# Gate and value by 16 block products for 18, over two token groups, with the tap products on ScalarE

## The chip, the cores and the metric

One Trainium2 chip, one core of it. The time is that of one execution on the device, in microseconds (us); a run gives several, and the median of the fast ones is quoted. The kernel before takes 3069 us, and its runs agree within 0.2%. The engines are named as in the profile: PE is TensorE's matmul, PEld its weight load, DVE is VectorE, ACT ScalarE, POOL GpSimd, SP SyncE, which here only starts DMAs (transfers between DRAM and the chip's memory). PSUM is the memory, in banks, in which TensorE adds up its products; reading a finished bank out is an eviction.

## The reference

A causal convolution with 7 taps, softmaxed for each of 8 heads, then an RMS norm and a SwiGLU layer without bias, on 8 sequences of 4096 tokens, 192 channels, 1536 inner columns, in fp32. The three weight matrices arrive as 64-bit floats; both kernels convert them to fp32 on the chip, once, by arithmetic on their 32-bit halves. This is the "conversion" of the start.

```python
# cut to what matters
w = softmax(weight, axis=-1)                         # (8 heads, 7 taps)
y[b, s, h*24:(h+1)*24] = sum_k w[h, k] * x_padded[b, s + k, h*24:(h+1)*24]
xn = y / sqrt(mean(y*y, axis=-1) + 1e-6) * rms_g      # 32768 tokens x 192
g, v = xn @ w_gate, xn @ w_val                        # 192 -> 1536 each
out = (silu(g) * v) @ w_out                           # 1536 -> 192
```

## The kernel before

A group is 512 tokens. The 192 channels are three blocks of 64, and TensorE works as two halves of 64 rows: the gate weights lie in the lower partitions, the value weights in the upper ones, so a gate product and a value product run side by side (the prediction shows the numbers).

```python
# cut to what matters
def load(g):                      # x of a group: a row of the tile holds 4 tokens and 6 before them
    ...
    src = bass.AP(tensor=row.tensor, offset=row.offset,
                  ap=[[NJ * D, P - first], [D, NJ + HALO], [1, D]])
    nc.sync.dma_start(out=t[first:, :, :], in_=src)     # first = 2 at the start of a sequence

# front(g), step by step beside the products of the group before
for k in range(K):                # both the tap products and the sums on VectorE (k = 0 only fills y)
    nc.vector.tensor_tensor(out=m[:], in0=xk, in1=w, op=ALU.mult)
    nc.vector.tensor_tensor(out=y[:], in0=y[:], in1=m[:], op=ALU.add)
...                               # squares, root, scaling, transpose, through DRAM

# inner(g): 12 column blocks, 3 channel blocks, gate and value
for c in range(NC):
    for ps, rows in ((gate, LOW), (val, UPP)):
        nc.tensor.matmul(out=ps[:], lhsT=w_in[rows, c, f * P : (f + 1) * P],
                         rhs=xg[rows, c, :], start=(c == 0), stop=(c == NC - 1))
nc.scalar.activation(out=sg[:], in_=gate[:], func=AF.Silu)
nc.vector.tensor_tensor(out=ht[:, f, :], in0=val[:], in1=sg[:], op=ALU.mult)

# outer(g, ht): 4 x 12 x 2 products of 192 columns, two evictions, one store
```

## Time and profile before

| | before |
|---|---|
| time, median | 3069.3 us |
| span of the profiled run | 3067.6 us |
| TensorE busy | 2990.7 us (97%) |
| VectorE, ScalarE, GpSimd busy | 51%, 20%, 3% |
| two groups (1024 tokens), steady | 93.0 us |
| first two groups done at | 179.7 us |

It is read from the top: who is busy, who is on the chain that ended last, at what rate the steady part runs, and what the start costs apart from that. The lines stand in the prediction below.

### The profile page before, as it was taken

What the parts mean: (1) busy time and instruction counts of PE and PEld (TensorE: products, weight loads), DVE (VectorE), ACT (ScalarE), POOL (GpSimd) and SP (SyncE); (2) the same over time, 40 slices, a digit from 0 to 9 for tenths busy, and PEclk for the clock granted to TensorE, in tenths of its full rate; (3) what the DMA queues carried; (4) which work ended last, traced back from release to release, by engine and by line L of the source; (5) the groups of instructions that cost most, each with busy time, mean ns of one, the idle gap of its engine ahead of it and who ended that gap; (6) DMA issues with size and microseconds to landing.
All of it is one profiled execution on the core that took longest, in us unless ns stands there. A gap on an engine that the chain in (4) does not pass through costs nothing.

```text
span 3067.6 us, 49649 instructions
## 1 busy us (share of the span) xinstructions
PE 2990.7 (97%) x21504; PEld 1896.0 (62%) x21504; DVE 1572.0 (51%) x2176; ACT 625.4 (20%) x1423; POOL 93.7 (3%) x163
## 2 busy tenths in 40 slices
PE   2799999999999999999999999999999999999999
PEld 1465665665665666666656656656656656666666
DVE  6745545446445455455455455454464454554552
ACT  1212122122122122122122121221221221221221
POOL 1000000000000000000000000000000000000000
PEclk9899999999999999999999999999999999999999
DMA  5221212211211211211211112112112112112111
GB/s 121 60 57 51 63 50 57 62 50 52 68 50 52 68 50 52 68 50 52 64 49 56 54 53 62 50 56 64 50 52 68 50 52 68 50 52 68 50 40 27
DMA packets 126731, 173.84 MB, mean 57 GB/s; under 512 B 9520, under 2 KB 91440, under 8 KB 126512
## 3 DMA queue, kind: packets, MB, share of 16 engines
q1 hardware_dynamic: 122880, 163.56, 19.2%
q0 software_dynamic: 1632, 4.72, 0.6%
q8 instruction: 168, 2.75, 0.4%
q10 hardware_dynamic: 2000, 2.39, 0.3%
q14 instruction: 51, 0.42, 0.0%
HBM read 120.31 MB, written 50.33 MB: 56 GB/s over the span
## 4 chain that ended last, share of the span: by engine, by line
PE 96%; DVE 3%; DMA 1%; issue 0%; POOL 0%; ACT 0%; DVEq 0%; SPq 0%; POOLq 0%
PE ps L284 63%; PE ps L302 32%; DMA x_sb<-in_x_dram 1%; DVE m L227 0%; DVE mf L184 0%; DVE sgn L183 0%; DMA raw_out<-in_moe_w_out_dram 0%; DVE y L228 0%; DVE w_in L192 0%; DVE exp L174 0%; DVE ht L290 0%; DVE exp L161 0%; DVE exp L171 0%; DVE sgn L179 0%; DVE man L166 0%
## 5 line engine op out<-in xcount | busy, mean ns | idle before, releaser
L284 PE MATMUL ps<-xT,w_in 64*128 64x512 f32 x9216 | 2002.3, 592 | 71.2 <-DVE sgn L179 47.9
L284 PEld LDWEIGHTS ps<-xT,w_in 64*128 64x128 f32 x9216 | 895.6, 188 | 1134.9 <-issue 1110.1
L302 PEld LDWEIGHTS ps<-wo_sb,ht 64*128 64x128 f32 x12288 | 1002.4, 187 | 31.6 <-issue 30.1
L302 PE MATMUL ps<-wo_sb,ht 64*128 64x192 f32 x12288 | 1009.6, 323 | 0.8 <-DVE wo_sb L189 0.8
L290 DVE TENSOR_TENSOR ht<-ps,sg 128x512 f32<-128x512 f32 x768 | 531.2, 692 | 546.1 <-ACT sg L289 529.2
L289 ACT ACTIVATE sg<-ps 128x512 f32<-128x512 f32 x768 | 458.4, 597 | 1419.0 <-PE ps L284 1410.2
L308 DVE TENSOR_TENSOR o_sb<-ps,o_sb 128x384 f32<-128x384 f32 x128 | 71.4, 558 | 909.0 <-ACT o_sb L307 909.0
L228 DVE TENSOR_TENSOR y<-y,m 128x768 f32<-128x768 f32 x384 | 368.1, 959 | 13.2
L227 DVE TENSOR_TENSOR m<-x_sb,taps 128x768 f32<-128x768 f32 x384 | 364.3, 949 | 0.0
L307 ACT COPY o_sb<-ps 128x384 f32<-128x384 f32 x128 | 61.3, 479 | 929.1 <-PE ps L302 929.1
L240 POOL TENSOR_SCALAR r<-ss 128x4 f32<-128x4 f32 x64 | 12.8, 199 | 2848.4 <-ACT sq L234 2848.4
L258 DVE STREAM_TRANSPOSE nt<-xn 128x768 f32<-128x768 f32 x64 | 99.1, 1548 | 0.0
L234 ACT ACTIVATE sq<-y 128x192 f32<-128x192 f32 x256 | 89.5, 350 | 21.1 <-DVE y L228 14.8
L248 DVE TENSOR_SCALAR xn<-y,r 128x192 f32<-128x192 f32 x256 | 63.8, 312 | 3.0 <-POOL r L243 3.0
L243 POOL TENSOR_TENSOR r<-r,nhalf 128x4 f32<-128x4 f32 x64 | 64.9, 1014 | 5.3
L224 DVE TENSOR_TENSOR y<-x_sb,taps 128x768 f32<-128x768 f32 x64 | 60.2, 941 | 0.0
L234 ACT ACTIVATION_READ_ACCUMULATOR sq<-y 128x1 f32 x256 | 47.6, 186 | 0.0
L170 ACT ACTIVATE mf<-man 128x768 f32<-128x768 uint32 (+1 forms) x12 | 8.2, 683 | 46.4 <-DVE man L166 46.4
L117 POOL DMA_DIRECT2D raw_in<-in_moe_w_val_dram x18 | 9.6, 540 | 40.0 <-DVE mf L184 39.2
L183 DVE TENSOR_TENSOR sgn<-exp,sgn 128x768 uint32<-128x768 uint32 (+1 forms) x12 | 9.1, 759 | 0.4
L76 DVE MEMSET x_sb<- 2x1152 f32 x8 | 8.1, 1018 | 2.3 <-issue 1.2
L192 DVE SCALAR_TENSOR_TENSOR w_in<-mf,rg_sb,sgn 128x256 f32<-128x256 f32 x18 | 7.7, 481 | 0.2
(26 smaller groups left out, 52.8 us busy)
## 6 DMA issues: line engine op xcount, KB each, us to landing
x_sb<-in_x_dram SPq DMA_DIRECT2D x56, 960.0 KB
xT<-xd SPq DMA_DIRECT2D x128, 384.0 KB
xd<-nt SPq DMA_DIRECT2D x256, 96.0 KB
out_dram<-o_sb SPq DMA_DIRECT2D x64, 384.0 KB
x_sb<-in_x_dram SPq DMA_DIRECT2D x8, 945.0 KB
raw_in<-in_moe_w_val_dram POOLq DMA_DIRECT2D x18, 128.0 KB, 7.8
raw_in<-in_moe_w_gate_dram ACTq DMA_DIRECT2D x18, 128.0 KB
raw_out<-in_moe_w_out_dram POOLq DMA_DIRECT2D x12, 192.0 KB, 4.1
```

Source lines behind the costliest of these rows:

```text
L227: nc.vector.tensor_tensor(out=m[:], in0=xk, in1=w, op=ALU.mult)
L228: nc.vector.tensor_tensor(out=y[:], in0=y[:], in1=m[:], op=ALU.add)
L234: nc.scalar.activation(out=sq[:], in_=y[:, j, :], func=AF.Square, accum_out=ss[:, j : j + 1])
L243: nc.gpsimd.tensor_tensor(out=r[:], in0=r[:], in1=nhalf[:], op=ALU.pow)
L248: nc.vector.tensor_scalar(out=n[:, j, :], in0=y[:, j, :], scalar1=r[:, j : j + 1], scalar2=None, op0=ALU.mult,)
L258: nc.vector.transpose(out=nt[:].rearrange("p c b j -> p c j b"), in_=n[:].rearrange("p j (c a) -> p c j a", a=Q),)
L284: nc.tensor.matmul(out=ps[:], lhsT=w_in[rows, c, f * P : (f + 1) * P], rhs=xg[rows, c, :], start=(c == 0), stop=(c == NC - 1),)
L289: nc.scalar.activation(out=sg[:], in_=gate[:], func=AF.Silu)
L290: nc.vector.tensor_tensor(out=ht[:, f, :], in0=val[:], in1=sg[:], op=ALU.mult)
L302: nc.tensor.matmul(out=ps[:, at], lhsT=ht[part, f, j * P : (j + 1) * P], rhs=wo_sb[part, f, :], start=(f == 0), stop=(f == FC - 1),)
L307: nc.scalar.copy(out=o2, in_=low[:, 0 : 2 * D])
L308: nc.vector.tensor_tensor(out=o2, in0=upp[:, 0 : 2 * D], in1=o2, op=ALU.add)
```

## The change

Two groups are taken together as a 2 x 3 array of blocks of x (A1 to A3, B1 to B3), and three column blocks of the weights as a 3 x 3 array. Their product needs 18 block products; a scheme of Strassen's kind needs 16, with sums of blocks of x (8 per pair of groups), sums of blocks of the weights (once, on GpSimd), and with partial sums that are read out of PSUM in the middle of their accumulation and used for several outputs. To make room on VectorE, which reads them, the tap products go to ScalarE, and the scalings by the root with them; four steps of the output weights' conversion go to GpSimd. The core, cut:

```diff
-    T = 512
-    NJ = T // P
+    T = 512
+    PT = 2 * T                       # tokens of a pair of groups
+    NJ = PT // P
 ...
     def load(p):
 ...
-            while first * NJ < HALO:
-                first += 1           # 2: the load is of 126 rows
+            first = 1                # the load is of 127 rows
 ...
     # front(p)
-            nc.vector.tensor_tensor(out=m[:], in0=xk, in1=w, op=ALU.mult)
+            for h in range(H):
+                nc.scalar.mul(m[:, :, hs], t[:, k : k + NJ, hs], taps[:, h, k : k + 1])
+                if h % 2:
+                    yield
             nc.vector.tensor_tensor(out=y[:], in0=y[:], in1=m[:], op=ALU.add)
 ...
+    def unit(u, side):               # 3 column blocks, both groups: 16 products in each half
+        mm(9, d, blk(B3), True)
+        side(1)
+        mm(12, c, cs(SS), True)
+        keep("e", c)                 # ScalarE copies a partial sum to SBUF, both halves
+        side(2)
+        mm(10, d, cs(W))
+        res(3, d, "e", op=ALU.add)   # VectorE: bank + copy, both halves
+        mm(3, a, blk(A3), True)
+        mm(5, a, cs(U))
+        keep("a", a)
+        mm(1, b, blk(A2), True)
+        mm(4, b, cs(U))
+        res(1, b, "a", rev=True)
+        ...                          # GpSimd adds output 3 to the copy "a", both halves
+        mm(13, d, cs(VS))            # the eighth product: into the bank that res(3) has read
+        keep("d2", d)
+        silu(3)
+        ...
 ...
     # main loop: what of the front part of the next pair stands where
+        elif s % 2 == 0:
+            step(nxt)                # in the units of a pair
+        ...
+        if 9 <= s <= 12:             # in its output stage
+            step(sums)               # block sums of x
+        else:
+            step(nxt, 2)
```

The load of x at the start of a sequence has 127 rows. The front part of the next pair has 47 steps, of which two are taken at each of 19 places of the output stage; the last nine are left to the units of the pair that follows.

## The prediction

> **What bounds the kernel now**
>
> I read the busy times first, then the chain that ended last, the groups, the chain in order of time, the timeline of two steady groups, and a table of windows over the start. Busy times, slices and chain, from the page:
>
> ```profile
> PE 2990.7 (97%) x21504; PEld 1896.0 (62%) x21504; DVE 1572.0 (51%) x2176; ACT 625.4 (20%) x1423; POOL 93.7 (3%) x163
> ...
> PE   2799999999999999999999999999999999999999
> ...
> PE 96%; DVE 3%; DMA 1%; issue 0%; POOL 0%; ACT 0%; DVEq 0%; SPq 0%; POOLq 0%
> ```
>
> TensorE is busy all the time after the second slice, and the chain says that it is also what sets the end. VectorE has half its time free, ScalarE four fifths. So fewer products are worth what they cost, as long as nothing else becomes the bound. The groups give the unit costs (columns: line, engine, operation, shapes, count, busy us, mean ns of one, idle before):
>
> ```profile
> L284 PE MATMUL ps<-xT,w_in 64*128 64x512 f32 x9216 | 2002.3, 592 | 71.2 <-DVE sgn L179 47.9
> ...
> L302 PE MATMUL ps<-wo_sb,ht 64*128 64x192 f32 x12288 | 1009.6, 323 | 0.8 <-DVE wo_sb L189 0.8
> L290 DVE TENSOR_TENSOR ht<-ps,sg 128x512 f32<-128x512 f32 x768 | 531.2, 692 | 546.1 <-ACT sg L289 529.2
> L289 ACT ACTIVATE sg<-ps 128x512 f32<-128x512 f32 x768 | 458.4, 597 | 1419.0 <-PE ps L284 1410.2
> ...
> L228 DVE TENSOR_TENSOR y<-y,m 128x768 f32<-128x768 f32 x384 | 368.1, 959 | 13.2
> L227 DVE TENSOR_TENSOR m<-x_sb,taps 128x768 f32<-128x768 f32 x384 | 364.3, 949 | 0.0
> L307 ACT COPY o_sb<-ps 128x384 f32<-128x384 f32 x128 | 61.3, 479 | 929.1 <-PE ps L302 929.1
> ...
> L258 DVE STREAM_TRANSPOSE nt<-xn 128x768 f32<-128x768 f32 x64 | 99.1, 1548 | 0.0
> L234 ACT ACTIVATE sq<-y 128x192 f32<-128x192 f32 x256 | 89.5, 350 | 21.1 <-DVE y L228 14.8
> ...
> L243 POOL TENSOR_TENSOR r<-r,nhalf 128x4 f32<-128x4 f32 x64 | 64.9, 1014 | 5.3
> ```
>
> The program has 4608 gate and value products and the page 9216, so each fp32 product is two instructions; two row halves run side by side, which is why the mean (592) exceeds busy time over count (217). The chain in order of time gives the steady rates:
>
> ```profile
> 1109.74 30.90 PE ps L284 x144
> ...
> 1838.14 15.60 PE ps L302 x192
> ```
>
> 30.90 / 144 = 0.2146 us for each gate or value instruction, 15.60 / 192 = 0.0813 for each output one. A group of 512 tokens takes 46.5 us, two take 93.0. The timeline of VectorE (start us, length us) shows its pitch:
>
> ```profile
> 1112.98 0.69 DVE L290 TENSOR_TENSOR ht<-ps,sg 128x512 f32<-128x512 f32 x1
> 1113.59 0.95 DVE L227 TENSOR_TENSOR m<-x_sb,taps 128x768 f32<-128x768 f32 x1
> 1114.57 0.96 DVE L228 TENSOR_TENSOR y<-y,m 128x768 f32<-128x768 f32 x1
> ```
>
> An operation that needs nothing of its predecessor starts 0.08 us before that one's end (pitch 0.61 for 512 elements); one that needs it starts 0.03 after. The windows 60 to 100 us (columns: PE, PEld, DVE, ACT, POOL, granted clock, DMA) show the start's price:
>
> ```profile
> 60.00:80.00 20.00, 14.15 (x52) 5.90 (x48) 19.59 (x36) 3.78 (x7) 2.66 (x5) 0.83 0.23 59
> 80.00:100.00 20.00, 10.49 (x30) 4.69 (x32) 19.58 (x35) 3.40 (x6) 3.75 (x7) 0.71 0.28 80
> ```
>
> There VectorE is full with the weights' conversion, TensorE waits and its clock falls. The first lasting matmul starts at 53.7 us, and the first two groups end at about 179.7 instead of 93.
>
> **What the Trainium skill says**
>
> "VectorE: DVE Perf Modes", section on the TRN2 errata, gives fp32 tensor_tensor (N+151)/0.96 ns: 691 for 512, and 957 for 768. The trace agrees: 692 and 959. "ScalarE: Activation LUTs", section "What ACT_TABLE_LOAD costs", gives 186 ns + 0.833 N, about 93 more for a per-partition scale, and 93 overlap back to back. For 192 elements that is 346; the trace has 350. A multiplication by a tap is then an estimated 0.44 us at a pitch of 0.35; no run here shows one yet. "GPSIMD Engine Reference", section 3.1, gives about 2.6 cycles per element for a two-input elementwise operation and 4497 ns for 2048; at 1.2 GHz an estimated 1.17 us for 512. The trace has none of that size. "TensorE: Matmul & The Clock Gate", Part 1, says that an idle window of about 3.4 us halves the clock; the falls to 0.83 and 0.71 above come with idle gaps of 3.7 to 5.9 us and agree.
>
> **The change part by part**
>
> 1. Products. A unit (three blocks of 128 gate and value columns, two token groups) has 16 products in each half instead of 18: 32 x 2 x 0.2146 = 13.73 us instead of 15.45. A pair of groups costs TensorE 4 x 13.73 + 2 x 15.60 = 86.1 instead of 93.0. Over 32 pairs that is 220 us, 7.2%, and the ceiling of the gain.
>
> 2. Reading partial sums. VectorE has 12 sums from PSUM and 6 products per unit, where it had 6 products: 18 x 0.61 = 11.0 us in 13.73. ScalarE has 10 copies (estimated 0.58 each, from 479 ns for 384) and 6 Silus: 9.4 us. Both fit, but they are now in a loop with TensorE, because the second product sum into a bank may not start before the first was read.
>
> 3. GpSimd's two sums per unit. They start when the first sum of res1 (the second pair that VectorE reads, ready when the seventh product ends, 6.0 us into the unit) is done, and the next VectorE product (mul3) waits for both: 2 x 1.17 = 2.35 us, with hops 2.45. The other VectorE work of the loop is 17 pitches and an end, 10.45 us. Loop: 12.9 us, below 13.73. So in a unit with nothing else TensorE stays the bound, with about 0.8 us to spare.
>
> 4. The front part. In the page VectorE's tap products (364 us plus 60) and scalings (64) go; ScalarE gets 56 multiplications (19.6 us at 0.35) and 8 scalings per pair. Sums stay on VectorE: 6 x 1.76 us. x block sums add 8 x 0.61 to 0.69. Nearly all of it lies in the output stage of 31.2 us: ScalarE about 24, VectorE about 18. It fits.
>
> 5. What spills over. The side steps are counted out: 38 of 47 front steps fall in the output stage, and the last six only after the last eviction. At the start of the next unit ScalarE evicts (to 0.5 us), does four tap products (1.9), VectorE adds (3.7), then six squares at 0.345 (5.9), and only then comes the copy that res3 needs: res3 ends at 7.7, where the eighth product wanted to start at 6.0. That is 1.7 us of wait. Then squares, the reciprocal root (1.0 on GpSimd, ahead of its two sums) and the eight scalings sit between ScalarE's copies, so mul3 starts at 11.3 instead of 9.2; from there VectorE runs without a gap, with six transposes, 3.3 us, among the sums. res3 of the second unit ends at about 25.0, where TensorE unhindered would want it at 13.73 + 6.0 = 19.7. So a pair loses 5.3 us, which later units cannot give back since TensorE is already full in them. Steady pair: 86.1 + 5.3 = 91.4 against 93.0.
>
> 6. The start. x of 1024 tokens is first (1.4 MB of 6.9 MB; the start before moved 216 to 227 GB/s), tap products from about 17 us, convolution to 39, squares, root and scalings to 46, conversion of the first three blocks to 52, transposes 55, through DRAM and back about 13: first product at about 68, not 54. In pair 0 VectorE has 8.2 us of conversion per unit, 5 of x sums, 14 of front and 10 of output weights beside its 11 per unit: units of about 30, 28, 26 and 14, an output stage of 31, and 8 for waits: pair 0 ends at about 205, where two groups ended at 179.7.
>
> Sum: 205 + 31 x 91.4 + 5 (last eviction and store, 5 before) = 3043.
>
> **The rivals**
>
> A. TensorE stays the bound everywhere and the spill is absorbed: 205 + 31 x 86.1 + 5 = 2879, 6% faster. For it: the busy sums of all engines fit under 86 us. Against it: the queues are in order and only two PSUM banks per running sum are there, so a late copy is a late product.
>
> B. VectorE and GpSimd become the bound in every unit. If a GpSimd sum takes 1.6 us or more, or VectorE's pitch on sums that wait for two engines is 0.70 and not 0.61, the loop is 14.4 us or more: 0.7 x 4 x 31 = 87 us on top, about 3130, slower at the edge. For it: nothing in the trace shows this GpSimd operation.
>
> C. ScalarE's tap products cost more than 0.35 us (24-element runs, a per-partition scale). At 0.44 the spill grows by about 2 us per pair, 62 us: 3105.
>
> D. The stalls of 2 to 3 us lower TensorE's clock as in the start. The gaps are shorter than those that did it, so I give it little.
>
> E. The expected transfers (1.5 MB back from DRAM per pair) delay the x sums. They are asked for at the start of the output stage and wanted 16 us later; hidden.
>
> **Range and chances**
>
> I keep the sum, rounded down slightly for the chance of A in part: 3035 us, 1% faster. The loss per pair is the weak term: each us of it is 31 us of time. A loss of 3 to 7 us makes 2972 to 3096, and the start adds 20 either way: range 2955 to 3105. The limit of 2% faster, 3008, needs a loss below 4.2 us, which I give 0.35; 2% slower, 3131, needs B or C in full, 0.09; within 2%, 0.56.
>
> **What would show it right or wrong**
>
> Right: gate and value instructions 8192 with busy near 1780 us; TensorE's idle time in front of them about 5 us per pair, in the first two units of a pair only, released by VectorE's res3, none in the third and fourth; GpSimd's sums near 1.17 us; tap products at 0.35 pitch; the first product at about 68 us. Wrong: idle time in all four units alike (B), an output stage longer than 31.2 us (C), a granted clock under 1 in the steady part (D), or hardly any idle time (A).

## The result, and the profile after

The changed kernel takes 3153.1 us (median of 4 runs) against 3069.3 us: a ratio of 1.0275 with a 95% interval of 1.0257 to 1.0293, 2.7% slower. Here and below a ratio is the mean time of one kernel's fast runs over that of the other's of the same rounds, so it is not quite the ratio of the medians quoted. All outputs are right. Where a run is set against the changed kernel (3153 us), that kernel ran in another call; the kernel before, which ran in all four calls, had medians of 3065.6 to 3069.3 us there.

Busy times, slices and chain of the kernel after, from its page:

```profile
PE 2901.5 (92%) x20480; PEld 2362.6 (75%) x20480; DVE 2130.6 (68%) x3214; ACT 2025.6 (64%) x4819; POOL 470.1 (15%) x445
...
PE   0369999999999999999999999999999999999999
...
PE 68%; ACT 12%; DVE 9%; issue 4%; POOL 3%; another core or an unknown queue 2%; DMA 0%; DVEq 0%; SPq 0%; POOLq 0%; ACTq 0%
```

TensorE still has the largest share, but the chain now runs through ScalarE and VectorE for a fifth of the span, and the first slice of TensorE is 0, the next two 3 and 6. A slice is 79 us: the kernel starts far later than before (there the row began 2, 7, 9). From the groups after (same columns as before):

```profile
L398 PE MATMUL ps<-xc,wf 64*128 64x512 f32 x5120 | 1659.7, 600 | 100.3 <-DVE sg L415 90.6
L398 PE MATMUL ps<-xb,wf 64*128 64x512 f32 x3072 | 1160.5, 609 | 144.3 <-DMA xb<-xd 123.6
...
L421 DVE TENSOR_TENSOR ht<-ht,sg 128x512 f32<-128x512 f32 x768 | 516.4, 682 | 281.4 <-POOL tp L448 281.4
...
L291 ACT ACTIVATE m<-x_sb,taps 128x192 f32<-128x192 f32 x1536 | 545.0, 442 | 0.0
...
L448 POOL TENSOR_TENSOR tp<-tp,sg 128x512 f32<-128x512 f32 x128 | 162.4, 1269 | 1173.8 <-DVE sg L415 1173.8
...
L291 ACT ACTIVATE y<-x_sb,taps 128x192 f32<-128x192 f32 x256 | 91.5, 440 | 67.8 <-DMA x_sb<-in_x_dram 67.8
```

The products are as counted, 5120 + 3072 = 8192. The last line holds the surprise: ScalarE's first tap product waited 67.8 us for x. The second line says the same of TensorE: 122 of the 123.6 us stand before its first product. The chain in order of time gives the steady period; here are the starts of the output stages of four pairs, the last two being the last but one and the last of the kernel:

```profile
1175.48 31.02 PE ps L496 x377
1268.12 31.02 PE ps L496 x377
...
3028.69 30.82 PE ps L496 x378
3114.75 31.09 PE ps L496 x378
```

A steady pair takes 92.66 us (from 248.67, the first output stage, to 3028.69, 30 pairs). The last pair, which has no next front part to carry, takes 86.06, the 86.1 that the products alone need. So the 7% of products are saved, and a pair loses again 6.6 of the 6.9 us that it gained.

That makes the whole account. The first pair ends at 279.6 us, where 205 was predicted: 75 too late. The other 31 take 30 x 92.66 + 86.06 = 2865.9, where 31 x 91.4 = 2833 was predicted: 32 too many. Together 107, and 3043 + 107 = 3150, the span. Of what was mis-sized, seven tenths is the first pair with its start.

### The profile page after: what moved, and what is told of

It is laid out like the page before. It is cut to its first block, busy times and chain, and to the rows that moved or that the text cites. A ratio compares the mean times of both kernels' runs of the same rounds, so it can differ in the third digit from the quotient of the medians.

```text
span 3150.4 us, 52944 instructions
## 1 busy us (share of the span) xinstructions
PE 2901.5 (92%) x20480; PEld 2362.6 (75%) x20480; DVE 2130.6 (68%) x3214; ACT 2025.6 (64%) x4819; POOL 470.1 (15%) x445
## 4 chain that ended last, share of the span: by engine, by line
PE 68%; ACT 12%; DVE 9%; issue 4%; POOL 3%; another core or an unknown queue 2%; DMA 0%; DVEq 0%; SPq 0%; POOLq 0%; ACTq 0%
PE ps L398 37%; PE ps L496 32%; ACT sq L302 4%; ACT tp L406 3%; DVE nt L326 2%; ACT y L314 2%; DVE sg L415 2%; ACT m L291 2%; DVE y L295 2%; DVE ht L415 2%; POOL r L311 2%; ACT sg L418 1%; DVE ht L421 1%; POOL wf L236 1%
## 5 line engine op out<-in xcount | busy, mean ns | idle before, releaser
L398 PE MATMUL ps<-xc,wf 64*128 64x512 f32 x5120 | 1659.7, 600 | 100.3 <-DVE sg L415 90.6
L398 PE MATMUL ps<-xb,wf 64*128 64x512 f32 x3072 | 1160.5, 609 | 144.3 <-DMA xb<-xd 123.6
L398 PEld LDWEIGHTS ps<-xc,wf 64*128 64x128 f32 x5120 | 882.6, 189 | 462.2 <-DVE sg L415 140.9
L406 ACT COPY tp<-ps 128x512 f32<-128x512 f32 x1280 | 700.8, 583 | 189.2 <-PE ps L398 184.3
L398 PEld LDWEIGHTS ps<-xb,wf 64*128 64x128 f32 x3072 | 546.7, 192 | 313.7 <-issue 180.5
L418 ACT ACTIVATE sg<-sg 128x512 f32<-128x512 f32 x768 | 487.4, 635 | 404.1 <-DVE sg L415 390.1
L421 DVE TENSOR_TENSOR ht<-ht,sg 128x512 f32<-128x512 f32 x768 | 516.4, 682 | 281.4 <-POOL tp L448 281.4
L291 ACT ACTIVATE m<-x_sb,taps 128x192 f32<-128x192 f32 x1536 | 545.0, 442 | 0.0
L415 DVE TENSOR_TENSOR sg<-ps,tp 128x512 f32<-128x512 f32 x640 | 436.4, 682 | 117.9 <-ACT tp L406 116.5
L415 DVE TENSOR_TENSOR ht<-ps,tp 128x512 f32<-128x512 f32 x640 | 433.8, 678 | 0.0
L291 ACT ACTIVATE y<-x_sb,taps 128x192 f32<-128x192 f32 x256 | 91.5, 440 | 67.8 <-DMA x_sb<-in_x_dram 67.8
```

Of the source, the lines that this page charges most:

```text
L291: nc.scalar.mul(m[:, :, hs], t[:, k : k + NJ, hs], taps[:, h, k : k + 1])
L398: nc.tensor.matmul(out=bank(h, bk)[:], lhsT=wf[u][rows, at[i], :], rhs=rhs, start=first, stop=True, skip_group_check=True,)
L406: nc.scalar.copy(out=t[:], in_=bank(h, bk)[:])
L415: nc.vector.tensor_tensor(out=dst, in0=in0, in1=in1, op=op)
L418: nc.scalar.activation(out=og[o][:], in_=og[o][:], func=AF.Silu)
L421: nc.vector.tensor_tensor(out=ov[o], in0=ov[o], in1=og[o][:], op=ALU.mult)
```

## The experiments

### Splitting the load of x

Theory 1: the 127 rows go through one of the 16 DMA engines. The sign was in the windows of the kernel after (columns: start and end, length, PE, PEld, DVE, ACT, POOL, granted clock, DMA share, GB/s):

```profile
60.00:70.00 10.00, 0.00 (x0) 0.00 (x0) 0.00 (x0) 0.00 (x0) 0.00 (x0) 1.00 0.06 27
```

No compute engine does anything for these 10 us, and the DMA engines are busy to 0.06, which is one of 16, moving 27 GB/s; the kernel before moved over 200 GB/s while it loaded. Theory 2: the load stands beside 5 MB of weights and waits its turn.

```diff
-        nc.sync.dma_start(out=t[first:, :, :], in_=src)            # rows 1 to 127: 127 rows
+        cuts = [first, first + 112, P] if first else [0, P]         # 112 rows and 15 rows
+        for lo, hi in zip(cuts, cuts[1:]):
+            ...
+            nc.sync.dma_start(out=t[lo:hi, :, :], in_=src)
```

> The changed kernel with one edit: at the start of a sequence the load of x, 127 rows of the tile in one DMA, becomes two, of 112 and of 15 rows. Theory 1 (rows share out badly: 127 is prime, so all of it goes through one of the 16 DMA engines; the trace shows a DMA share of 0.06 = 1/16 and 27 GB/s while only that load is left): the first tap product starts at about 15 to 25 us and not 72.4, the first matmul at 65 to 75 and not 122.4, and the time falls by 45 to 60 us, to about 3095 to 3108. Theory 2 (the load is slow because 5 MB of weights are asked for at the same moment on the same queues): nothing moves by more than 5 us, about 3150.

Measured: 3094.0 us, ratio to before 1.0088 (1.0073 to 1.0103), so 59 us less than the changed kernel. The windows and the timeline of this run:

```profile
10.00:20.00 10.00, 0.00 (x0) 0.00 (x0) 1.55 (x1) 7.21 (x21) 2.59 (x6) 1.00 1.05 246
```

```profile
12.79 2.87 ACT L293 ACTIVATE y<-x_sb,taps 128x192 f32<-128x192 f32 x8 [6.30 <-DMA x_sb<-in_x_dram]
...
62.48 2.04 PE L400 MATMUL ps<-xb,wf 64*128 64x512 f32 x2 [62.48 <-DMA xb<-xd]
```

The DMA engines are all at work (share 1.05), the tap products start at 12.8 us and not 72.4, the first matmul at 62.5 and not 122.4. The same bytes and the same neighbours; what differs is that one DMA of 127 rows became two of 112 and 15. That it is the rows and not the second DMA, the run on the kernel before will show. The time fell 59 us where 45 to 60 were expected, to 3094, 1 us below the range of times given with it. All of it is at the start: the other seven sequences begin with such a load too, but in the kernel after every pair between the first and the last took 92.6 to 92.9 us.

### The weights on another queue

```diff
-    load_in(0, nc.sync)
-    load_in(1, nc.sync)
+    load_in(0, nc.scalar)
+    load_in(1, nc.scalar)
```

> The changed kernel, its x load left as one DMA of 127 rows, but the weights of the first two units asked for from ScalarE's queue and not from SyncE's, behind the x load. Theory 1 (127 rows on one DMA engine): the first tap product still starts at 65 to 75 us, time within 10 us of 3153. Theory 2 (the queue shared with the weights delays x): the first tap product starts at 15 to 40 us and the time falls by 30 us or more.

Measured: 3161.8 us (one run). The time moved by 9 us, within what theory 1 allowed, but the first tap product came at 81.9 and not between 65 and 75. It was not x that it waited for: issuing the weights kept ScalarE's queue until 79.4, and the taps' own exponential stands behind that. x must be read from the windows:

```profile
50.00:60.00 10.00, 0.00 (x0) 0.00 (x0) 0.00 (x0) 0.00 (x0) 0.00 (x0) 1.00 0.06 27
60.00:70.00 10.00, 0.00 (x0) 0.00 (x0) 0.00 (x0) 0.00 (x0) 0.00 (x0) 1.00 0.06 26
```

One engine is still at it alone, and finer windows of the same trace (not shown) have that share, 0.05 to 0.08, up to 76 us and 0.01 from 76 to 78: by this sign x landed no sooner than in the kernel after. So SyncE's queue, shared with the weights, was not the cause, but the run is a weaker witness than it was meant to be.

### A prime number of rows in the kernel before

```diff
-        nc.sync.dma_start(out=t[first:, :, :], in_=src)             # 126 rows
+        cuts = [first, first + 113, P] if first else [0, P]          # 113 rows and 13 rows
```

> The kernel before, in which the load of x at the start of a sequence, 126 rows in one DMA, is cut into 113 rows (a prime) and 13. Theory 1 (a prime number of rows goes through one engine): 113 rows of 7680 bytes, 0.87 MB at about 25 GB/s, need some 35 us, where all of 126 rows had landed by 22 us; the first product of the convolution then starts at about 37 us and not 22.1, the first matmul some 10 to 20 us later than 53.7, and the time grows by 10 to 20 us. Theory 2 (number of rows does not matter): 3069 as before, first product of the convolution at 22.

Measured: 3096.1 us (one run) against 3066.7. A window and the first tap product:

```profile
30.00:40.00 10.00, 0.00 (x0) 0.00 (x0) 0.00 (x0) 0.00 (x0) 0.00 (x0) 1.00 0.06 26
```

```profile
48.68 0.96 DVE L226 TENSOR_TENSOR y<-x_sb,taps 128x768 f32<-128x768 f32 x1 [23.15 <-DMA x_sb<-in_x_dram]
```

The tap products started at 48.7 us, not 22.1 and not the 37 expected, the first lasting matmul at 80.2 and not 53.7. So the kernel before gets 29 us slower by nothing but how the rows of one load are divided: two DMAs again, and this time slower. The direction and the kind are theory 1's. The size was underestimated: the load took longer than its bytes at 26 GB/s. That the 113 rows first shared their engine with the weights is likely, and not shown.

### Moving the transposes

Theory A: the front part that spills into the first two units holds up VectorE's queue at bad places. In the steady part of the kernel after, the timeline of VectorE shows such a place:

```profile
1228.86 0.67 DVE L421 TENSOR_TENSOR ht<-ht,sg 128x512 f32<-128x512 f32 x1
1229.46 1.56 DVE L326 STREAM_TRANSPOSE nt<-y 128x256 f32<-128x256 f32 x3
1230.86 0.68 DVE L421 TENSOR_TENSOR ht<-ht,sg 128x512 f32<-128x512 f32 x1
1231.45 0.68 DVE L415 TENSOR_TENSOR sg<-ps,tp 128x512 f32<-128x512 f32 x1
1232.05 0.68 DVE L415 TENSOR_TENSOR ht<-ps,tp 128x512 f32<-128x512 f32 x1
```

and that of TensorE who waits for it (in the bracket: idle time before, and what ended it):

```profile
1214.35 1.29 PE L398 MATMUL ps<-xc,wf 64*128 64x512 f32 x3 [1.55 <-DVE sg L415]
...
1232.18 1.29 PE L398 MATMUL ps<-xc,wf 64*128 64x512 f32 x3 [1.21 <-DVE sg L415]
```

The second is the eighth product of the second unit, released 0.05 us after the first half of res3 ended at 1232.13. Both stand where the prediction put them, in the first two units of a pair and nowhere else. The idle gaps themselves are only 2.8 us of the 6.6: the rest does not show as idle, as TensorE's products in between are spread out (11 instructions in 3.35 us at 1217.46; in the third unit of the pair before, 10 such take 2.47 at 1156.38).

```diff
-                elif s % 2 == 0:
+                elif (u == 0 and s % 2 == 0 and s <= 12) or (u, s) in ((1, 8), (2, 8), (2, 10)):
                     step(nxt)
```

> The changed kernel, with the six transposes of the front part taken out of the end of the first unit and put three each behind the pair of sums after which VectorE waits for GpSimd, in the second and in the third unit of a pair; all else as it was. Theory A (what spills over out of the output stage holds up VectorE's queue at bad places): the transposes fill a wait of 2 us, so the wait for res3 in the second unit shrinks by about 3 us a pair; a pair takes about 89.4 us and not 92.66, the time falls by 31 x 3.2 = 100 us to about 3055. Theory B (VectorE's total work in the units is what counts, wherever it stands): no change, 3150.

Measured: 3075.0 us, ratio 1.0027 (1.0010 to 1.0043), 78 us less than the changed kernel. A pair takes 90.05 us: 2.6 less, of the 3.2 expected. The transposes did not go away, they moved into the wait for GpSimd:

```profile
1128.18 0.68 DVE L415 TENSOR_TENSOR ht<-tp,ps 128x512 f32<-128x512 f32 x1
1128.78 1.58 DVE L326 STREAM_TRANSPOSE nt<-y 128x256 f32<-128x256 f32 x3
1130.90 0.69 DVE L421 TENSOR_TENSOR ht<-ht,sg 128x512 f32<-128x512 f32 x1 [0.54 <-POOL tp L448]
```

VectorE's wait there, in the third unit, was 2.0 us and is 0.54. In the stretch shown of the steady part, the gap at the second unit's eighth product is gone. Theory B, that only the sum of VectorE's work counts, falls.

### Two tiles for the squares

In the kernel after, a square starts 0.485 us after the last one; in the kernel before 0.345. The difference in the source is that all squares go to one throw-away tile.

```diff
-        sq = work.tile([P, D], F32, name="sq")
+        sqs = [work.tile([P, D], F32, name=f"sq{i}") for i in range(2)]
         for j in range(NJ):
+            sq = sqs[j % 2]
```

> The changed kernel in which the squares are written to two tiles in turn and not to one. In the changed kernel a square starts 0.485 us after the last one, in the kernel before, with two tiles, 0.345. If the one tile is why, and the squares lie on the path into the first unit of each pair, six of them get 0.84 us shorter there: 31 x 0.84 = 26 us less, about 3127. If the gap has another cause, or the squares are not on the path, 3153.

Measured: 3127.0 us, ratio 1.0198 (1.0184 to 1.0212), 26 us less, as expected. A pair takes 91.81, 0.85 less. TensorE's first gap shrinks from 1.55 to 0.84 us. So the squares lie on the path into the first unit, as step 5 of the prediction had it, and the prediction's 0.345 was the wrong pitch for them.

### A third GpSimd operation

```diff
+        nc.gpsimd.tensor_tensor(out=sb["a", 0][:], in0=sb["a", 0][:], in1=ones[:], op=ALU.mult)
         for h in range(2):
             ...
             nc.gpsimd.tensor_tensor(out=sb["a", h][:], in0=sb["a", h][:], in1=o3, op=ALU.add)
```

> The changed kernel with one more GpSimd operation in each unit, a product of the same size by ones, ahead of its two sums (the result stays the same). If the loop of VectorE and GpSimd has only the 0.7 us to spare that VectorE waits in the third unit, 1.27 us more make each unit about 0.6 us longer: 124 units x 0.6 = 75 us and about 0.7 more in each first and second unit, 31 x 2 x 0.7 = 43; in all about 3230 to 3270. If GpSimd stands beside the loop, 3153.

Measured: 3214.6 us (one run), 61 us more, where 77 to 117 were expected. A steady pair takes 94.51 us, 1.85 more; the last, without a front part, 87.66, 1.60 more. So GpSimd's two sums do stand in the loop. In the third unit VectorE's wait for GpSimd grew by 1.35 us (2.01 to 3.36), and the fourth unit's GpSimd work came 14.24 us after the third's, where it was 13.74: of 1.35 us, 0.50 reached the unit, so an undisturbed unit had about 0.85 us to spare. Rival B needed more than the sums cost.

```profile
1049.13 1.81 PE L400 MATMUL ps<-xc,wf 64*128 64x512 f32 x3 [1.56 <-DVE sg L417]
1067.83 1.29 PE L400 MATMUL ps<-xc,wf 64*128 64x512 f32 x3 [1.22 <-DVE sg L417]
```

These are the eighth products of the first and the second unit, 18.70 us apart; in the kernel after, above, they are 17.83 apart. The 0.87 us between says that in the first unit, with the front part's work in it, less was to spare: GpSimd's queue lies on the path to the second wait, as step 5 of the prediction had it. The other 0.98 of the 1.85 is about twice the 0.50 of an undisturbed unit; the second unit, where 0.7 extra was expected, added no more than that.

### The front part spread otherwise

If the spilled steps are the loss, none of them may stand in the way. Eight steps go into the second to fourth unit of the pair before, where ScalarE idles; 36 into the output stage, most of them where ScalarE had been waiting for the next eviction; the transposes into VectorE's wait for GpSimd.

```diff
+    EARLY = ((1, 13), (1, 15), (2, 6), (2, 13), (2, 15), (3, 6), (3, 13), (3, 15))    # unit, place
+    OUTER = {s: 2 for s in range(8)}
+    OUTER.update({8: 4, 9: 1, 10: 1, 11: 1, 12: 1, 13: 3, 14: 2, 15: 2, 16: 1, 17: 1, 18: 2, 19: 1})
+        early = front(p + 2)
-                elif s % 2 == 0:
+                elif (u, s) in ((0, 8), (1, 8), (1, 10)):
                     step(nxt)
+                if (u == 3 and s % 2 == 0) if p == 0 else (u, s) in EARLY:
+                    step(early)
-        nxt = front(p + 2)
+        nxt = early
-            else:
-                step(nxt, 2)
+            step(nxt, OUTER.get(s, 0))
```

The split load is in it too.

> The changed kernel with the x load of a sequence's start in two DMAs (112 and 15 rows), and with the front part spread otherwise: two of its tap passes in the second to fourth unit of the pair before, where ScalarE waits; squares, root and scalings all inside the output stage; three transposes each in the first and second unit, in VectorE's wait for GpSimd. Theory A (the loss per pair is the front part that spills over into the first units): the loss of 6.6 us a pair falls to 0 to 1, a pair takes 86.1 to 87, and with the 59 us of the split load the time is 3153 - 59 - 31 x 6 = about 2890 to 2930, 4 to 6% faster than the kernel before. Theory B (the loop of TensorE, VectorE and GpSimd is itself too long, spilled work or not): a pair keeps 90 us or more, time 3030 or more.

Measured: 2918.1 us, ratio 0.9515 (0.9502 to 0.9528). Two output stages of its chain, one pair apart:

```profile
277.21 30.82 PE ps L498 x378
364.02 30.82 PE ps L498 x378
```

Over the run a pair takes 86.82 us: 5.8 of the 6.6 are back. The kernel is 4.9% faster than before, with every product, sum and copy of the change in it.

### The output weights converted on VectorE

The first pair of the kernel after takes 157 us from the first matmul (122.4) to the end of its output stage (279.6), of which 137 was predicted. GpSimd is busy for 85 of the 126 us of its four units, TensorE's clock is 0.84 there:

```profile
122.00:248.00 126.00, 86.33 (x255) 50.47 (x257) 96.03 (x135) 67.04 (x157) 85.28 (x96) 0.84 0.12 37
```

As said above, the change had moved four steps of the output weights' conversion to GpSimd, into the one queue with the block sums of the weights and with the two sums of each unit.

```diff
-            yield from convert(nc.gpsimd, raw.pop(("out", i)), exp_o[:], mf_o[:], dst)
+            yield from convert(nc.vector, raw.pop(("out", i)), exp_o[:], mf_o[:], dst)
```

> The changed kernel, in which the four steps of the output weights' conversion that ran on GpSimd run on VectorE instead. In the changed kernel these steps take 1.2 to 1.9 us each on GpSimd, in one queue with the block sums of the weights and with the two sums per unit, and VectorE waits for them in the first pair. Theory A (GpSimd's queue is what makes the first pair long): VectorE gets 6 x 1.75 = 10 us more, but waits of some 25 us go; the first pair (first matmul to the end of its output stage, 157 us in the changed kernel) is 10 to 20 us shorter, the time falls to 3133 to 3143. Theory B (VectorE's own work makes the first pair long): 10 us more, 3163.

Measured: 3140.1 us, ratio 1.0237 (1.0223 to 1.0251), 13 us less. The first pair takes 145 us (122.7 to 268.0). More work on VectorE made it shorter, as theory A has it. It is still 8 above the predicted 137; what that rest is made of was not taken apart.

### All of it together

> The kernel with the front part spread otherwise and the x load split (2918 us), and with the output weights converted on VectorE and the squares in two tiles. If the first pair gets 10 to 20 us shorter there too, and the squares are no longer on the path: 2898 to 2908, 5.2 to 5.5% faster than the kernel before. If VectorE's own work makes the first pair long: 2928.

Measured: 2883.7 us, ratio 0.9401 (0.9388 to 0.9414): 6.0% faster than the kernel before, and 14 us below the range. The expectation was wrong about the squares: it held them to be off the path. The chain of this run, the last three output stages:

```profile
2674.12 30.90 PE ps L499 x379
2760.25 30.90 PE ps L499 x379
2846.39 31.09 PE ps L499 x378
```

86.13 us a pair, the same as the products alone (86.06): the last 0.7 us of each pair went as well (31 x 0.69 = 21 us), beside 14 us from the first pair (its end is at 207.2 us, 221.6 with only the respread front). The conversion stands in the first pair alone, so the 0.7 us of the later ones are put down to the squares' tiles; no run had these on top of the respread front alone. This version beats both.

## Why the prediction was wrong

It said 3035 us, within 2% as the likeliest, and the range of 2955 to 3105 does not hold 3153.

- Step 1, the products, was right: 8192 instructions, and 86.06 us for a pair with no front part. Their busy time is 1924 us, though, and not near 1780 as the prediction's signs had it. Of the excess about 31 us lie in the first pair (86.33 busy in its units, for 4 x 13.73), and an estimated 3.8 in each steady pair (6.6 lost, 2.8 idle), where products are spread out without showing as idle.
- Step 2 was right: VectorE's sums at a pitch of 0.60 us, ScalarE's copies at 0.58 us each.
- Step 3 was right in kind. GpSimd's sums took 1.27 us, not the 1.17 estimated, and the loop still had about 0.85 us to spare in an undisturbed unit (third_pool). Rival B was not the cause; units three and four run without a gap. Its sum was wrong too: sums of 1.6 us give a loop of 2 x 1.6 + 0.1 + 10.45 = 13.75 us, level with TensorE's 13.73, and not the 14.4 that a pitch of 0.70 gives.
- Step 4 was right: 48 tap products in 16.67 us at the start are 0.347 us each (0.442 long), so rival C falls. The output stage stayed at 31.
- Step 5 was right in mechanism and place, and its size was off: 6.6 us a pair, not 5.3. The squares were taken at 0.345 us instead of 0.485, worth 0.85 us a pair (two_squares); the root takes 1.66 us for eight columns where the four of before took 1.01, and the GpSimd sums are longer by 0.1 each, ahead of the same wait of VectorE (2.79 us at mul3 in the first unit); what these two cost a pair was not measured alone. That the place of the transposes costs 2.6 of the 6.6 us was shown (transposes_later), and so was that all of the loss is the spill (respread and the last version). In all it cost 32 us against the prediction.
- **Step 6 failed**, and decides the case: "x of 1024 tokens is first (1.4 MB of 6.9 MB; the start before moved 216 to 227 GB/s), tap products from about 17 us". It gave x its share of all 16 engines' rate. The 127 rows had one engine, and the tap products started at 72.4 us. Everything behind it came 54 us late: the first product at 122.4, not 68. The rest of the step, from the tap products to the first product, was 51 us as predicted and 50 in the run. The Trainium skill has the rule: "DMA: Bandwidth & Descriptors", in the section on why a DMA increments its semaphore by 16, says that a DMA is spread over the largest number of engines up to 16 that divides the slowest dimension of both its sides, and names 127 partitions as a case of one engine. The trace agrees (DMA share 0.06, 27 GB/s), as do the split load (59 us) and the kernel before with 113 rows (29 us). The diff showed the 126 rows becoming 127; the prediction does not mention it.
- Step 6 was also wrong by 20 us on the first pair: "8 for waits" was too little. Moving the conversion steps off GpSimd's queue takes 12 us of that back (157 to 145).
- Rival D, a lower clock through stalls, is not seen in the steady part: the windows over the two stalls show 1.00. In the first pair, with gaps of up to 5.9 us, the clock was 0.84, as at the start before.
- Rival E did not come up in the steady part. Yet a transfer did decide the case, at the start, for which the prediction allowed 20 us either way and listed no rival.
- Two more sums are loose. A loss of 3 to 7 us with 20 us of start either way is 2952 to 3116, wider than the 2955 to 3105 given; and C in full comes to 3105, short of the 3131 that the chance of "slower" was hung on. The measured 3153 is above all of them.

With only the load of x mended, by the split, the kernel takes 3094 us: inside the range, 0.9% slower than before. There the first product comes at 62.5 us, 5.5 sooner than predicted, and the first pair is as long as ever.

## What to carry to other kernels

When a change alters the number of rows of a DMA, look at its divisors: with two DMAs of 112 and 15 rows the first tap product started 60 us sooner than with one of 127. When an engine has time to spare on average, ask where in its queue the added work stands: the same front part cost 6.6 us a pair at the head of the units and nothing in the waits of the engines that carry it. A change that saves work and ends slower may only be placed badly: with the placement mended this one is 6% faster.

## What the Trainium skill lacked or had wrong

- "GPSIMD Engine Reference", section 4.1 (engine selection), calls one-input operations on GpSimd roughly line-rate. The conversion's tensor_scalar on 128x384 uint32, one input and two operations on it, took at least 1.50 us on GpSimd and 1.86 us as the mean of one group, where the same step took 0.43 us on VectorE (out_on_vector); on fp32, a sign change of 128x128 took 0.53 us and a two-input sum of that size 0.45 (medians, kernel after).
- No page gives the cost of GpSimd's power operation: 1.01 us for 4 columns (kernel before), 1.66 us for 8 (kernel after).
- "ScalarE: Activation LUTs" gives the overlap of activations back to back, but not that squares with an accumulator output start 0.485 us apart when they write one tile and 0.345 us apart when they take turns between two, which was worth 26 us here.
